# Row copies of k and q on other engines, and batch 0 ordered tile by tile, in an attention and feed-forward kernel

## The chip, the cores and the metric

The kernel runs on one NeuronCore of a Trainium2 chip. The core has TensorE (PE; PEld is its weight load), VectorE (DVE), ScalarE (ACT), GpSimd (POOL) and SyncE (SP), each with an instruction queue of its own that runs in order, and 16 DMA engines that all queues share. The metric is the device time of one execution in microseconds (us). The kernel before took a median of 387.32 us in three runs (386.34 to 393.78).

## What is computed

```python
# q, k, v: [8, 12, 448, 64] float32; w_in: [768, 2048]; w_out: [2048, 768]
scores = matmul(q, k.transpose(0, 1, 3, 2)) / sqrt(64) - log(448)
attn = 1 / (1 + exp(-scores))                  # a sigmoid, no softmax
x = matmul(attn, v).transpose(0, 2, 1, 3).reshape(8 * 448, 768)
h = x @ w_in
out = (h * (1 / (1 + exp(-h)))) @ w_out        # [3584, 768] float32
```

## The kernel before

**Quads, tiles, batches.** A quad is four of a batch's twelve heads, so there are 24 quads g, three (`NQ`) per batch. A quad has seven tiles (`NCH`) of 64 keys of each of its heads; `units` lists all 168 (g, ch) in order. For each tile `scores` (L171) makes four matmuls, with 64x64 of kT as weights and 448 columns of qT as the moving operand, into two PSUM banks (`psc`, two buffers in the pool `ps_sc`, L178), and then one sigmoid on ScalarE, 128x896, into `attnT` (L185). `values(g)` (L195) multiplies a quad's seven `attnT` tiles by v in 28 matmuls into two PSUM tiles `pav`, and VectorE writes them to `xT` (L220). A batch's feed-forward part needs the `xT` of its three quads.

**Feed-forward.** `h_unit(b, fc)` (L229) makes one of 16 tiles of h for a batch: six matmuls into `ph`, a sigmoid `tsig` on ScalarE (L245) and a multiplication `gTr` on VectorE (L246). The first four of the six need only the batch's first two quads. `out_set` (L286) multiplies two blocks of gTr by w_out with seven products in place of eight, with the sums and differences of blocks `S` (L315 to L323) and of quarters of w_out. The latter (`w_sums`, L264, L275) are 16 VectorE subtractions, 14 of which run one by one behind the h tiles 2 to 15 of batch 1. All of this is one generator, `stream`; each step is about one matmul and yields the time that it stands for.

**PSUM.** `ps_1` has four one-bank buffers for everything but the scores: `ph`, `po`, `pav`, `ptr` and the dummies `pw`.

**k and q transposed.** Scores need k and q with the head dimension on the partitions. Quads 0 to 5 are transposed by TensorE (`pe_transpose`, L141; 28 small matmuls against an identity, four pieces, each copied out of PSUM by VectorE, L156). Quads 6 to 23 go through `dma_transpose` (L160): GpSimd copies the rows of k and q into another order (`kr`, `qr`, 128x896 each, two buffers each in `p2`; L164), and SyncE issues a DMA transpose of each copy (L165). The results have four buffers in `p4`.

**Loads and stores.** GpSimd issues the loads of q, k, v and both weights, which change float32 to float16 on the way (L79, L109, L116). `kf` and `qf` have four buffers, `vf` five. SyncE issues nearly all stores of the output (L296).

**The loop (L473 to L505).** It walks over `units` in bursts of two tiles. Behind the burst's scores come the values of a quad whose last tile went by in an earlier burst, then perhaps the TensorE transposes of a quad to come, and then either dummy matmuls (`keep_busy`, in batch 0, up to four a burst; eight more run at the very start) or `stretch(ns)`, which takes steps from `stream` worth that many ns. Two h tiles of batch 0 are begun early (`early`, four matmuls each, L483 to L485). In front of tile 42, where batch 2 begins, one long `stretch(18500)` runs nearly all h tiles of batch 1. Loads and transposes by DMA hang on two hooks: `after_transpose(5)` makes the row copies of quads 6 and 7, `after_values(4)` those of quad 8, and `after_values(g)` from 5 on those of g + 4.

Of the kernel before, what the change touches and what calls it, by code (L numbers as in the profile page):

```python
# [10 lines left out]
F16 = mybir.dt.float16  # L11
# [6 lines left out]
def kernel(  # L18
# [9 lines left out]
    nc = tc.nc  # L28

    B, H, S, D = q.shape  # L30
    NT, DMODEL = out.shape
    DFF = moe_w_in.shape[1]
    P = 128
    HP = P // 2
    NCH = S // HP
# [36 lines left out]
    def load(names, g, c0=0, c1=NCH):  # L72
        b, iq = divmod(g, NQ)
        for name in names:
            if (name, g) not in flat:
                new_flat(name, g)
            for half in range(2):
                h0 = half * (H // 2) + 2 * iq
                nc.gpsimd.dma_start(  # L79
                    flat[name, g][half * HP : (half + 1) * HP, :, c0:c1].rearrange(  # L80
                        "p i c d -> p i (c d)"
                    ),
                    source[name][b, h0 : h0 + 2].rearrange("i (p c) d -> p i (c d)", c=NCH)[
                        :, :, c0 * D : c1 * D
                    ],
                )
# [38 lines left out]
    def new_qkT(g):  # L125
        for name in ("k", "q"):
            qkT[name, g] = p4.tile([P, NCH, P], F16, tag=f"{name}T", name=f"{name}T")
# [3 lines left out]
    def keep_busy(n):  # L131
        if n == 0:
            return
        pw = ps_1.tile([P, 512], F32, tag="ps1", name="pw")
        for _ in range(n):
            nc.tensor.matmul(pw, dummy[:, :P], dummy, start=True, stop=True)
# [4 lines left out]
    def pe_transpose(g, pieces=(("k", 0, 4), ("k", 4, NCH), ("q", 0, 4), ("q", 4, NCH))):  # L141
        if ("k", g) not in qkT:
            new_qkT(g)
        for name, c0, c1, *copy in pieces:
            dst = qkT[name, g].rearrange("p c t -> p (c t)")
            ptr = ps_1.tile([P, 512], F32, tag="ps1", name=f"ptr{name}")
            for c in range(c0, c1):
                for j in range(2):
                    nc.tensor.matmul(  # L149
                        ptr[j * D : (j + 1) * D, (c - c0) * P : (c - c0 + 1) * P],  # L150
                        flat[name, g][:, j, c, :],
                        ident,
                        start=True,
                        stop=True,
                    )
            (copy[0] if copy else nc.vector.tensor_copy)(  # L156
                dst[:, c0 * P : c1 * P], ptr[:, : (c1 - c0) * P]
            )

    def dma_transpose(g):  # L160
        new_qkT(g)
        for name in ("k", "q"):
            rows = p2.tile([P, NCH, 2, D], F16, tag=f"{name}r", name=f"{name}r")
            nc.gpsimd.tensor_copy(rows, flat[name, g].rearrange("p j c d -> p c j d"))  # L164
            nc.sync.dma_start_transpose(  # L165
                out=qkT[name, g], in_=rows.rearrange("p c j d -> p (c j d)")
            )

    attnT = {}

# [21 lines left out]

    part_of = {}

    def values(g, rounds=NCH):  # L195
        b, iq = divmod(g, NQ)
        if iq == 0:
            assert b < 2 or b - 2 in h_done
            xT[b] = p2.tile([P, NPAIR, S], F16, tag="xT", name="xT")
        pav, done_rounds = part_of.pop(g, None) or (  # L200
            [ps_1.tile([P, 512], F32, tag="ps1", name="pav") for _ in range(2)],
            0,
        )
        for ch in range(done_rounds, rounds):
            at = attnT.pop((g, ch))
            for half in range(2):
                own = slice(half * HP, (half + 1) * HP)
                for j in range(2):
                    nc.tensor.matmul(  # L209
                        pav[half][j * D : (j + 1) * D, :S],  # L210
                        flat["v", g][own, j, ch, :],
                        at[own, j, :],
                        start=(ch == 0),
                        stop=(ch == NCH - 1),
                    )
        if rounds < NCH:
            part_of[g] = pav, rounds
            return
        for half in range(2):
            nc.vector.tensor_scalar_mul(xT[b][:, half * NQ + iq, :], pav[half][:, :S], SX)  # L220
        if iq == NQ - 1:
            ready.add(b)
# [6 lines left out]
    def h_unit(b, fc):  # L229
        ph = ps_1.tile([P, 512], F32, tag="ps1", name="ph")  # L230
        for at, cc in enumerate(pairs):
            assert b in ready or at < 4
            nc.tensor.matmul(  # L233
                ph[:, :S],
                w_in_sb[:, cc, fc * P : (fc + 1) * P],
                xT[b][:, cc, :],
                start=(at == 0),
                stop=(at == NCC - 1),
            )
            if at < NCC - 1:  # L240
                yield 189
        if fc == NFC - 1:
            h_done.add(b)
        tsig = p3.tile([P, S], F16, tag="tsig", name="tsig")
        nc.scalar.activation(tsig, ph[:, :S], AF.Sigmoid, bias=0.0, scale=ISX)  # L245
        nc.vector.tensor_mul(  # L246
            gTr[:, fc, (b % 2) * S : (b % 2) * S + S], ph[:, :S], tsig
        )
        yield 189
# [36 lines left out]
    def out_set(a1, rows1, a2, rows2, last=False):  # L286
# [60 lines left out]
            store(rows1, osb[0], whole, (nc.sync, nc.sync))  # L347
        yield 163

    early = [h_unit(0, fc) for fc in range(2)]  # L350
    sums = w_sums()

    def moe_h(b):
        for fc in range(NFC):
            yield from early[fc] if b == 0 and fc < 2 else h_unit(b, fc)
            if b == 1 and fc >= 2:
                next(sums)

    def moe_set(m, g):
        step = out_set(block(g), row_blocks(m, g), block(g + 1), row_blocks(m, g + 1))  # L360
# [27 lines left out]
    def stretch(ns):  # L388
        nonlocal done, due
        due += ns  # L390
        while done < due:
            step_ns = next(stream, None)
            if step_ns is None:
                break
            done += step_ns
# [23 lines left out]
    def after_transpose(g):  # L419
        if g == 0:  # L420
            load("kq", 4)
            load_w_in(2)
            load("v", 3)
        elif g == 1:
            load("kq", 5)
            load_w_in(3)
            load("v", 4)
        elif g == 4:
            load("kq", 8)
            load("v", 6)  # L430
            load("v", 7)
        elif g == 5:
            load("v", 8)
            load("kq", 9)
            dma_transpose(6)
            dma_transpose(7)

    def after_values(g):
        if g == 0:
            load("v", 5)  # L440
            for nh in range(2):
                for part in range(2):
                    load_w_out(nh, part)
        elif g == 2:
            load("kq", 6)
            load("kq", 7)
        elif g == 4:
            load("kq", 10)
            load("kq", 11)
            dma_transpose(8)  # L450
            load("v", 9)
        elif g > 4:
            if g + 4 < NQB:
                dma_transpose(g + 4)
            if g + 5 < NQB:
                load("v", g + 5)
            if g + 7 < NQB:
                load("kq", g + 7)

    def values_if_any():  # L460
        if waiting:
            g = waiting.pop(0)
            values(g)
            after_values(g)
# [3 lines left out]
    keep_busy(1)  # L468
    pe_transpose(0, (("q", 0, 4), ("q", 4, NCH, act_copy), ("k", FIRST, NCH)))
    after_transpose(0)  # L470
    transposed = 1
    paces = {1: 1600, 2: 2200, 3: 2550, 4: 3400, 5: 3400, 6: 3000, 7: 3000}
    for n in range(0, len(units), 2):  # L473
        burst = units[n : n + 2]
        spare = 4 if n < 1.5 * NT_B else 0
        if n == 2 * NT_B:
            values_if_any()
            stretch(18500)
        elif n == NT_B + 1:
            values_if_any()  # L480
        for u in burst:
            scores(*u)
            if u[0] == NQ - 1 and u[1] >= NCH - 3 and u[1] % 2 == 0:  # L483
                for _ in range(4):
                    next(early[(u[1] - NCH + 3) // 2])  # L485
                if u[1] == NCH - 1:
                    values(u[0], NCH - 1)
        if waiting:
            spare = 0
        values_if_any()  # L490
        for g, ch in burst:
            if ch == NCH - 1:
                waiting.append(g)
        if transposed < 2 * NQ and n + 4 >= transposed * NCH - 1:
            pe_transpose(transposed)
            after_transpose(transposed)
            transposed += 1
            spare = 0
        if 0 not in ready:
            keep_busy(spare if n < NT_B - 3 else 0)  # L500
        else:
            stretch(paces[1] if 1 not in ready else paces[n // NT_B])
    for g in waiting:
        values(g)
    for _ in stream:  # L505
# [31 lines left out]
```

## Time and profile before

The profiled execution took 387.83 us; its span, from the first to the last instruction, is 386.1 us. All times below are of this execution.

| what | us |
|---|---|
| span | 386.1 |
| sigmoids of scores (L185), 168, mean 1005 ns | 159.5 busy on ACT |
| h matmuls (L233), 768 | 154.3 busy on PE |
| gTr (L246), 128, mean 622 ns | 77.8 busy on DVE |
| tsig (L245), 128, mean 546 ns | 67.6 busy on ACT |
| row copies (L164), 36, mean 1007 to 1035 ns by name (medians 1007 and 1006) | 37.0 busy on POOL |
| w_out differences (L275), 16 | 15.6 busy on DVE |
| issue of loads on POOL (L79), 144 | 88.2 |
| DMA transposes, issue to landing: least, median, most | 2.9, 3.3, 11.5 |

Lines of the profile name an engine, a line of the kernel, the tile written and the tile read, the shape and a count. A matmul's mean duration (353 ns for ph) is from its issue to its end; matmuls overlap, so the time that one takes in a row of them is read from a row's length over its count. In brackets stands how long the engine had been idle before, and what ended that. In a chain of waits each piece is what the next one waited for; "issue" is time for which the profile shows no wait. In tables by stretch each engine's busy time is followed by its number of instructions; the column behind POOL is the clock that the throttle granted to TensorE, 1.00 being full.

### The profile page before, as it was taken

The page shows a single profiled execution, that of the slowest core. Times are in us where ns is not written, and L with a number is a line of the kernel's source. Part 1 is how long each engine was busy: PE and PEld are TensorE (multiplying, and loading weights), DVE is VectorE, ACT ScalarE, POOL GpSimd, SP SyncE. Part 2 cuts the span into 40 slices and gives each one's busy share as a digit, 9 for nine tenths or more (in the row PEclk, how much of TensorE's full clock was granted, in tenths as well). Part 3 has the DMA queues.
Part 4 walks back from the last instruction along what each step waited for, and adds up shares of the span by engine and source line. Part 5 has one row for each costly group of instructions (what it writes and reads, how often), then busy time and mean ns, then how long its engine had stood idle before and what let it go on. Part 6 is the DMA issues. An engine that isn't in the chain of part 4 may idle for free.

```text
span 386.1 us, 7648 instructions
## 1 busy us (share of the span) xinstructions
PE 372.3 (96%) x3089; PEld 186.7 (48%) x3089; DVE 228.1 (59%) x385; ACT 235.4 (61%) x322; POOL 126.5 (33%) x194
## 2 busy tenths in 40 slices
PE   7898999879999999999999999999999999999995
PEld 2444444434554444544555544544455444555663
DVE  2445646998775446454667444644466445756774
ACT  4989885456865887577454487568774687044000
POOL 8937418954655514523505505303000000000000
PEclk9999999999999999999999999999999999999999
DMA  7999999999987937836569745452202300120233
GB/s 113 184 198 205 203 204 194 149 154 170 223 169 132 170 57 120 154 63 106 73 132 171 125 106 74 73 130 28 45 17 68 82 2 1 22 63 0 65 101 82
DMA packets 66403, 42.71 MB, mean 111 GB/s; under 512 B 37056, under 2 KB 62912, under 8 KB 66368
## 3 DMA queue, kind: packets, MB, share of 16 engines
q0 software_dynamic: 28032, 22.69, 40.6%
q1 hardware_dynamic: 38112, 19.31, 23.7%
q8 instruction: 24, 0.39, 0.4%
q10 hardware_dynamic: 224, 0.23, 0.2%
q14 instruction: 11, 0.09, 0.1%
HBM read 45.61 MB, written 11.01 MB: 147 GB/s over the span
## 4 chain that ended last, share of the span: by engine, by line
PE 86%; ACT 5%; DVE 5%; issue 2%; DMA 1%; POOL 1%; ACTq 0%; DVEq 0%; POOLq 0%
PE ph L233 34%; PE po L303 33%; PE psc L178 9%; PE pav L209 8%; ACT attnT L185 4%; DVE gTr L246 2%; DVE w_out_sb L275 1%; DVE T L275 1%; DMA kf<-in_k_dram 1%; ACT tsig L245 1%; DVE kT L156 0%; POOL qf L79 0%; PE ptrk L149 0%; DVE S L315 0%; DVE osb L311 0%
## 5 line engine op out<-in xcount | busy, mean ns | idle before, releaser
L185 ACT ACTIVATE attnT<-psc,bias_s 128x896 f16<-128x896 f32 x168 | 159.5, 1005 | 57.5 <-PE psc L178 57.2
L233 PE MATMUL ph<-xT,w_in_sb 128*128 128x448 f16 x768 | 154.3, 353 | 2.9 <-DVE gTr L246 2.7
L246 DVE TENSOR_TENSOR gTr<-ph,tsig 128x448 f16<-128x448 f32 x128 | 77.8, 622 | 82.3 <-ACT tsig L245 81.9
L233 PEld LDWEIGHTS <-w_in_sb 128*128 128x128 f16 x768 | 71.7, 98 | 79.8 <-issue 18.0
L245 ACT ACTIVATE tsig<-ph 128x448 f16<-128x448 f32 x128 | 67.6, 546 | 52.9 <-PE ph L233 48.7
L79 POOL DMA_DIRECT2D vf<-in_v_dram x48 | 28.9, 616 | 113.0 <-PE pav L209 69.4
L303 PEld LDWEIGHTS <-S 128*128 128x128 f16 x448 | 42.3, 98 | 34.1 <-issue 5.4
L311 DVE SCALAR_TENSOR_TENSOR osb<-po,osb 128x384 f32<-128x384 f32 x70 | 37.6, 554 | 27.4 <-PE po L303 27.2
L178 PE MATMUL psc<-qT,kT 64*64 64x448 f16 x672 | 50.2, 362 | 2.4 <-ACT attnT L185 2.0
L220 DVE TENSOR_SCALAR xT<-pav 128x448 f16<-128x448 f32 x48 | 27.7, 619 | 32.3 <-PE pav L209 32.3
L303 PE MATMUL po<-T,S 128*128 128x384 f16 x224 | 39.8, 326 | 0.9 <-DVE S L315 0.9
L303 PE MATMUL po<-w_out_sb,S 128*128 128x384 f16 x224 | 40.3, 326 | 0.0
L303 PEld LDWEIGHTS <-gTr 128*128 128x128 f16 x304 | 28.5, 98 | 23.8 <-issue 6.0
L209 PE MATMUL pav<-attnT,vf 64*64 64x448 f16 x672 | 36.5, 350 | 0.4 <-DVE gTr L246 0.4
L303 PE MATMUL po<-w_out_sb,gTr 128*128 128x384 f16 x192 | 34.7, 326 | 0.0
L79 POOL DMA_DIRECT2D kf<-in_k_dram x48 | 29.4, 635 | 9.4 <-PE ph L233 3.8
L79 POOL DMA_DIRECT2D qf<-in_q_dram x48 | 29.9, 654 | 7.5 <-PE ph L233 3.5
L178 PEld LDWEIGHTS <-kT 64*64 64x64 f16 x672 | 13.8, 104 | 32.9 <-issue 31.2
L209 PEld LDWEIGHTS <-vf 64*64 64x64 f16 x672 | 19.9, 107 | 12.8 <-issue 1.9
L311 DVE SCALAR_TENSOR_TENSOR osb<-po,m 128x384 f32<-128x384 f32 x42 | 23.1, 551 | 3.6 <-PE po L303 2.7
L318 ACT ACTIVATE m<-po 128x384 f32<-128x384 f32 x14 | 6.9, 492 | 24.2 <-PE po L303 23.7
L303 PE MATMUL po<-T,gTr 128*128 128x384 f16 x112 | 21.5, 327 | 0.0
(38 smaller groups left out, 157.0 us busy)
## 6 DMA issues: line engine op xcount, KB each, us to landing
out_dram<-osb SPq DMA_DIRECT2D x54, 192.0 KB, 3.0
qf<-in_q_dram POOLq DMA_DIRECT2D x48, 112.0 KB, 5.1
vf<-in_v_dram POOLq DMA_DIRECT2D x48, 112.0 KB, 4.3
kf<-in_k_dram POOLq DMA_DIRECT2D x46, 112.0 KB, 4.5
w_in_sb<-in_moe_w_in_dram POOLq DMA_DIRECT2D x4, 768.0 KB, 10.8
w_out_sb<-in_moe_w_out_dram POOLq DMA_DIRECT2D x4, 768.0 KB, 15.1
kT<-kr SPq DMA_TRANSPOSE x18, 3.3
qT<-qr SPq DMA_TRANSPOSE x18, 3.3
```

The lines of the kernel that those rows point to most:

```text
L79: nc.gpsimd.dma_start(flat[name, g][half * HP : (half + 1) * HP, :, c0:c1].rearrange("p i c d -> p i (c d)"), source[name][b, h0 : h0 + 2] ...
L178: nc.tensor.matmul(psc[own, j, :S], qkT["k", g][rows, ch, own], qkT["q", g][rows, :, own], start=True, stop=True,)
L185: nc.scalar.activation(attnT[g, ch], psc[:, :, :S], AF.Sigmoid, bias=bias_s, scale=QKSCALE)
L209: nc.tensor.matmul(pav[half][j * D : (j + 1) * D, :S], flat["v", g][own, j, ch, :], at[own, j, :], start=(ch == 0), stop=(ch == NCH - 1),)
L220: nc.vector.tensor_scalar_mul(xT[b][:, half * NQ + iq, :], pav[half][:, :S], SX)
L233: nc.tensor.matmul(ph[:, :S], w_in_sb[:, cc, fc * P : (fc + 1) * P], xT[b][:, cc, :], start=(at == 0), stop=(at == NCC - 1),)
L245: nc.scalar.activation(tsig, ph[:, :S], AF.Sigmoid, bias=0.0, scale=ISX)
L246: nc.vector.tensor_mul(gTr[:, fc, (b % 2) * S : (b % 2) * S + S], ph[:, :S], tsig)
L275: nc.vector.tensor_sub(o[:, f : f + 2], x[:, f : f + 2], y[:, f : f + 2])
L303: nc.tensor.matmul(po[:, :NO2], a[:, fc, :], w[:, fc, :], start=(fc == 0), stop=(fc == NHC - 1))
L311: nc.vector.scalar_tensor_tensor(out=o, in0=po, scalar=sign, in1=x, op0=ALU.mult, op1=ALU.add)
L318: nc.scalar.activation(m1, po, AF.Copy, scale=ISX)
```

## The change

- `dma_transpose` takes a quad, one of the two names and the copy to use. GpSimd makes no row copies any more.
- Quads 6, 7 and 8 are copied by ScalarE, k and q one after the other, behind the h tiles 4, 7 and 10 of batch 1 (`by_h1`), with the load of k and q of the quad four on behind each pair.
- Quads 9 to 23 are copied by VectorE. From `after_values(6)` on they are put on a list, `later`, and each burst takes one copy from it, behind the burst's values; the load of k and q of the quad four on follows the copy of q.
- The first 24 tiles are no longer run in bursts of two. Behind the scores of each tile stands what a table, `behind`, lists for it: dummies, the transposes of k or of q of a quad, two or three tiles' share of a quad's values, or two matmuls of an early h tile. The transposes of quads 1 to 3 come ahead of the values of quads 0 to 2. `values` can stop at any tile and go on later, as before. Behind tile 23 a stretch follows, and then the loop of two-tile bursts as before. The loop's dummies in batch 0 go from 16 to 9.

```diff
-    def dma_transpose(g):
-        new_qkT(g)
-        for name in ("k", "q"):
-            rows = p2.tile([P, NCH, 2, D], F16, tag=f"{name}r", name=f"{name}r")
-            nc.gpsimd.tensor_copy(rows, flat[name, g].rearrange("p j c d -> p c j d"))
-            nc.sync.dma_start_transpose(
-                out=qkT[name, g], in_=rows.rearrange("p c j d -> p (c j d)")
-            )
+    def dma_transpose(g, name, copy):
+        if ("k", g) not in qkT:
+            new_qkT(g)
+        rows = p2.tile([P, NCH, 2, D], F16, tag=f"{name}r", name=f"{name}r")
+        copy(rows, flat[name, g].rearrange("p j c d -> p c j d"))
+        nc.sync.dma_start_transpose(
+            out=qkT[name, g], in_=rows.rearrange("p c j d -> p (c j d)")
+        )
...
+    by_h1 = {4: 6, 7: 7, 10: 8}
...
     def moe_h(b):
         for fc in range(NFC):
             yield from early[fc] if b == 0 and fc < 2 else h_unit(b, fc)
-            if b == 1 and fc >= 2:
-                next(sums)
+            if b == 1:
+                if fc >= 2:
+                    next(sums)
+                if fc in by_h1:
+                    for name in ("k", "q"):
+                        dma_transpose(by_h1[fc], name, act_copy)
+                    load("kq", by_h1[fc] + 4)
...
     def after_transpose(g):
...
         elif g == 5:
             load("v", 8)
             load("kq", 9)
-            dma_transpose(6)
-            dma_transpose(7)
...
     def after_values(g):
...
-        elif g == 4:
-            load("kq", 10)
-            load("kq", 11)
-            dma_transpose(8)
-            load("v", 9)
-        elif g > 4:
-            if g + 4 < NQB:
-                dma_transpose(g + 4)
-            if g + 5 < NQB:
-                load("v", g + 5)
-            if g + 7 < NQB:
-                load("kq", g + 7)
+        elif g >= 4 and g + 5 < NQB:
+            load("v", g + 5)
+        if g >= 6:
+            for to in (9, 10) if g == 6 else (g + 4,):
+                if to < NQB:
+                    later.extend(((to, "k"), (to, "q")))
+
+    later = []
+
+    def rows_if_any():
+        if later:
+            g, name = later.pop(0)
+            dma_transpose(g, name, nc.vector.tensor_copy)
+            if name == "q" and g + 4 < NQB:
+                load("kq", g + 4)
...
+    behind = {
+        1: ((keep_busy, 2),),
+        2: ((keep_busy, 1),),
+        3: ((transposes, 1, "k"),),
+        4: ((transposes, 1, "q"),),
+        5: ((keep_busy, 2),),
+        6: ((keep_busy, 2),),
+        7: ((keep_busy, 2),),
+        8: ((transposes, 2, "k"),),
+        9: ((transposes, 2, "q"),),
+        10: ((rounds, 0, 2),),
+        11: ((rounds, 0, 4),),
+        12: ((rounds, 0, 7),),
+        13: ((transposes, 3, "k"),),
+        14: ((transposes, 3, "q"),),
+        15: ((rounds, 1, 2),),
+        16: ((rounds, 1, 4),),
+        17: ((rounds, 1, 7),),
+        18: ((begin, 0),),
+        19: ((begin, 1),),
+        20: ((rounds, 2, 2),),
+        21: ((begin, 0), (rounds, 2, 4)),
+        22: ((rounds, 2, 7),),
+        23: ((begin, 1),),
+    }
+    for n in range(NT_B + 3):
+        scores(*units[n])
+        for do, *what in behind.get(n, ()):
+            do(*what)
+
+    transposed = NQ + 1
     paces = {1: 1600, 2: 2200, 3: 2550, 4: 3400, 5: 3400, 6: 3000, 7: 3000}
-    for n in range(0, len(units), 2):
+    stretch(paces[1])
+    for n in range(NT_B + 3, len(units), 2):
         burst = units[n : n + 2]
-        spare = 4 if n < 1.5 * NT_B else 0
         if n == 2 * NT_B:
             values_if_any()
             stretch(18500)
-        elif n == NT_B + 1:
-            values_if_any()
         for u in burst:
             scores(*u)
-            if u[0] == NQ - 1 and u[1] >= NCH - 3 and u[1] % 2 == 0:
-                for _ in range(4):
-                    next(early[(u[1] - NCH + 3) // 2])
-                if u[1] == NCH - 1:
-                    values(u[0], NCH - 1)
-        if waiting:
-            spare = 0
         values_if_any()
+        rows_if_any()
```

`transposes` calls `pe_transpose` for the two pieces of one name and, behind q, `after_transpose`; `rounds(g, end)` is `values(g, end)`, with `after_values(g)` at the end of a quad; `begin(fc)` takes two steps of an early h tile.

More of the change, by code (lines that the diff above doesn't have):

```diff
@@ L193, with values @@
     part_of = {}
-    def values(g, rounds=NCH):
+    def values(g, end=NCH):
         b, iq = divmod(g, NQ)
-        if iq == 0:
+        if b not in xT:
             assert b < 2 or b - 2 in h_done
@@ L203, in values @@
         )
-        for ch in range(done_rounds, rounds):
+        for ch in range(done_rounds, end):
             at = attnT.pop((g, ch))
@@ L215, in values @@
                     )
-        if rounds < NCH:
-            part_of[g] = pav, rounds
+        if end < NCH:
+            part_of[g] = pav, end
             return
@@ L470, with transposes, rounds, begin @@
     after_transpose(0)
-    transposed = 1
+    def transposes(g, name):
+        pe_transpose(g, ((name, 0, 4), (name, 4, NCH)))
+        if name == "q":
+            after_transpose(g)
+    def rounds(g, end):
+        values(g, end)
+        if end == NCH:
+            after_values(g)
+    def begin(fc):
+        for _ in range(2):
+            next(early[fc])
+    behind = {
[28 more added lines that the diff above has]
+    transposed = NQ + 1
     paces = {1: 1600, 2: 2200, 3: 2550, 4: 3400, 5: 3400, 6: 3000, 7: 3000}
-    for n in range(0, len(units), 2):
+    stretch(paces[1])
+    for n in range(NT_B + 3, len(units), 2):
         burst = units[n : n + 2]
-        spare = 4 if n < 1.5 * NT_B else 0
         if n == 2 * NT_B:
@@ L497 @@
             transposed += 1
[L498 to L502, printed above, removed]
+        stretch(paces[1] if 1 not in ready else paces[n // NT_B])
     for g in waiting:
```

## The prediction, made before the changed kernel ran

> **What bounds the kernel now.** I read the page's busy times first, then busy times by stretch, then the chain of waits, then the order in time of the two places where the stretches show a hole. Times are microseconds. The profiled execution took 387.83: its span of 386.1 and 1.73 around it. It is 0.5 over the median of the runs shown, 387.32, and inside their 386.34 to 393.78; the sum below is made on 387.83.
>
> ```profile
> PE 372.3 (96%) x3089; PEld 186.7 (48%) x3089; DVE 228.1 (59%) x385; ACT 235.4 (61%) x322; POOL 126.5 (33%) x194
> ```
>
> TensorE is busy for 96% of the span, no other engine for over 61%. By stretch (busy time of PE, PEld, DVE, ACT, POOL, then clock and DMA):
>
> ```profile
> 7.80:31.80 24.00, 21.63 (x296) 10.76 (x292) 10.12 (x19) 22.68 (x26) 16.55 (x27) 1.00 1.21 188
> 59.80:86.70 26.90, 23.29 (x136) 11.26 (x133) 25.15 (x36) 13.23 (x22) 22.66 (x34) 1.00 1.33 164
> 86.70:381.90 295.20, 295.13 (x2336) 149.73 (x2336) 175.00 (x301) 173.38 (x240) 69.89 (x103) 1.00 0.48 90
> ```
>
> From 86.7 on TensorE has 0.07 of idle time in 295.20: nothing can be won there by waits, and whatever starts the last stretch earlier ends the kernel earlier by as much. The holes are batch 0 (ACT is busy 22.68 of 24.00) and 59.8 to 86.7 (VectorE is busy 25.15 of 26.90). The chain of waits in the second (start, length, what):
>
> ```profile
> 59.83 7.50 PE ph L233 x39
> ...
> 68.55 0.55 DVE T L275
> 69.10 3.11 issue
> 72.21 0.61 DVE gTr L246
> ...
> 76.32 2.44 DVE w_out_sb L275
> ...
> 86.01 0.61 DVE S L315
> ...
> 86.67 1.83 PE po L303 x10
> ```
>
> From 67.9 to 86.67 the chain runs on VectorE. The order in time says why:
>
> ```profile
> 68.21 1.05 POOL L164 COPY kr<-kf 128x896 f16<-128x896 f16 x1
> 68.47 3.81 DVE L275 TENSOR_TENSOR T<-w_out_sb 128x768 f16<-128x768 f16 x1
> 72.87 4.80 PE L233 MATMUL ph<-xT,w_in_sb 128*128 128x448 f16 x24 [1.02 <-DVE gTr L246]
> 76.24 2.52 DVE L275 TENSOR_TENSOR w_out_sb<-w_out_sb 128x768 f16<-128x768 f16 x1
> 76.37 1.11 POOL L164 COPY kr<-kf 128x896 f16<-128x896 f16 x1
> 79.35 2.24 PE L233 MATMUL ph<-xT,w_in_sb 128*128 128x448 f16 x11 [1.68 <-DVE gTr L246]
> ```
>
> A subtraction that takes 0.54 elsewhere takes 3.81 while GpSimd makes four row copies in a row (68.21 to 71.86), and 2.52 beside the next two; TensorE then waits 1.02 and 1.68 for gTr. In batch 0:
>
> ```profile
> 7.83 9.19 ACT L185 ACTIVATE attnT<-psc,bias_s 128x896 f16<-128x896 f32 x10 [0.61 <-PE psc L178]
> 28.61 2.80 ACT L185 ACTIVATE attnT<-psc,bias_s 128x896 f16<-128x896 f32 x3 [0.85 <-PE psc L178]
> 28.73 1.16 DVE L220 TENSOR_SCALAR xT<-pav 128x448 f16<-128x448 f32 x2 [2.76 <-PE pav L209]
> 31.79 0.57 PE L178 MATMUL psc<-qT,kT 64*64 64x448 f16 x8
> ```
>
> Ten sigmoids run back to back at 0.919; 24 of them from 7.83 would end at 29.89, and end at 31.41. ACT lost 1.52 to scores that came late, and the h matmuls wait for xT, ready at 29.89.
>
> **Row copies away from GpSimd.** From 59.83 to 86.67 TensorE has this work: 99 ph matmuls at 0.189 (96 in 18.16 late in the chain) = 18.71, 16 po at 0.163 (168 in 27.31) = 2.61, two score groups at 0.50 = 1.00, and four changes between them at 0.11 (18 ph beside scores take 3.51 against 3.40) = 0.44; together 22.8 of 26.84. The hole is worth 4.1 and is the most that this edit can give. It opens fully only if VectorE keeps up: without GpSimd's copies its turn per h tile is gTr 0.54 and the subtraction 0.47 in the chain, 1.01 against six matmuls = 1.13. It does, by a tenth.
>
> In the place of GpSimd's ten copies in this stretch come six on ACT, ahead of the tsig of tiles 5, 8 and 11 of h(1). ACT copies of this shape are not in the trace. Nearest: 128x512 from SBUF 0.632 (L364), and from L245's 448 elements in 0.546 to L185's 896 in 1.005 it is 1.02 ns an element; so an estimate of 1.02, and 0.93 behind another, as the sigmoids overlap: 1.95 a pair. Behind the pair wait tsig, then gTr, then the PSUM buffer that TensorE needs. A tile takes 1.2 from its last matmul to the end of gTr (0.54 and 0.62, with gaps), and its buffer is needed again after three more tiles, 3.4: cover for 2.2. One pair fits. Per three tiles ACT has 1.95 and three tsig at some 0.5, 3.45 against 3.4, so the three pairs hardly add up; with VectorE catching up I charge 0.4, and 0.2 for S (L315) behind the last gTr. Bounds: nothing, and all three pairs uncovered, 5.9. I stay near the low end because the cover is counted from rows. Term: 4.1 - 0.6 = **3.5**.
>
> SP has the transposes of quads 6 to 8 at once before the stores; quad 6's first landed after 3.9. Quad 6 is copied near 66 and its scores come near 78, so some 6 are spare. kq 10 to 12 on POOL now wait for the ACT copies; behind them are only loads for later batches.
>
> Thirty copies go to VectorE after 90, one a burst, after xT. Their price is not in the trace: 428 ns for 128x512 from f32 (L414) below, GpSimd's 1007 above; 0.5 taken, 15 in all of 295 with VectorE at 175. TensorE waits for VectorE in none of that stretch, so this counts nothing; uncovered it would be at most 30 times 0.5. What sits behind each copy is a gTr or osb whose buffer has three more tiles of time. In return the S additions lose GpSimd (L323 1033 ns between 90 and 270, 681 after it); also off the path. A copy waits for the transposes of two quads before, which landed within 11.5; the quads are some 14 apart.
>
> A rule speaks against VectorE here. The Trainium skill (SBUF — State Buffer, "SBUF: two separate sides") says that a VectorE copy in a two-port mode locks GpSimd out, so that a DMA issued there stretches from about 620 to 3100 ns. By that, as an estimate, thirty copies could cost POOL 74; no run here shows it, and the sum would stay as it is, since POOL is idle for two thirds of the span.
>
> **Batch 0 tile by tile.** Transposes of quads 1 to 3, values and early h matmuls are the same work, one piece behind each tile's scores. The largest usual piece, 12 value matmuls at 47 ns (28 in 1.32) = 0.57, with scores at 0.25 makes 0.82 of the sigmoid's 0.919; one place (two h matmuls and eight values) is some 0.1 over, covered by the second score buffer. So ACT should run unbroken. Scores of tile 22 then start when sigmoid 20 ends, 7.83 + 21 x 0.919 = 27.13; with 0.38 and 0.57 the values end at 28.08, xT 1.2 later at 29.3 against 29.89; one of the nine h matmuls that waited now goes ahead. The scores of tile 24 come at 30.9 or so, not 31.79. Term: **0.8**; bounds 1.5 (all that ACT lost) and -1.0 (as many new late scores as before). Loads allow it: w_in's first quarter, issued at 13.73 and landed 8.8 later, is needed at 23.9. Sixteen dummies of the loop become nine; they only fill.
>
> From 31.8 to 59.8 and after 86.7 the order of the path is as before. Sum: 387.83 - 3.5 - 0.8 = **383.5**.
>
> **Rivals.** *ACT takes GpSimd's place.* If a pair takes over 2.2 (1.1 a copy), TensorE waits instead; wholly uncovered the stretch takes 22.8 + 5.9 = 28.7 against 26.84, and with 0.8 from batch 0 the time is 388.9, slower than before. For it: ACT's balance is 3.45 to 3.4. Against: four buffers. 13%.
>
> *The clock.* The first eight dummies take 3.26, 0.41 each; from 7.90 four take 1.04, though the clock reads 1.00 in both. If fewer dummies bring that rate back in batch 0, a piece of 0.82 becomes 1.64, 0.7 over the sigmoid, in some 17 tiles: +12, 399. It decides once matmuls of batch 0 run at twice their time. Against: real work takes the dummies' place at much the same density. 4%. The Trainium skill (TensorE: Matmul & The Clock Gate, Part 1) has half rate return after an idle window of some 3.4; by that the price would be nothing, as no hole in the plan is so long.
>
> *Half an effect.* VectorE's margin of 0.12 a tile is spent on late tsig, so that the chain stays on it, or batch 0's new order loses what it gains: 385.5 to 387.8. 18%.
>
> *More.* Over 2% needs 8, and the holes hold 4.1 + 1.5; only something unseen gives it. 5%.
>
> **How the numbers follow.** The forecast has 60%, 383.5 (382.2 to 385 for its own bounds). Eight in ten: from 381.0 (near all of both holes, and a run 0.5 quicker, as the median is) to 387.6. Two per cent of 387.32 is 7.7, about what this measurement tells from no change: faster 5%, slower 6% (the clock, and a bad end of the ACT case), within 89%.
>
> **What would show it.** L275 at some 0.55 a piece with no 2 to 4 among them; no TensorE wait for gTr over 0.5 between 59 and 83; 24 sigmoids in one run from 7.8 to about 30; POOL busy some 37 less; ACT copies at 1.0. Wrong if TensorE waits for tsig beside the ACT copies, if 60 to 87 still takes over 25, or if scores wait in batch 0.

## The result, and the profile after

The changed kernel takes a median of 389.9 us (17 runs, 386.64 to 391.57) beside 387.53 for the kernel before (17 runs): a ratio of 1.0054, 95% interval 1.0032 to 1.0077. It is slower, by 2.1 us by this ratio, where the prediction had 383.5, 3.8 below the median that it knew. Ratios leave out executions over 1.5% above the fastest of their kernel; medians do not. The profiled execution took 390.17 with a span of 388.4. Every difference between two spans below is one between single profiled executions; medians and ratios are from the timed runs.

Busy times of the changed kernel, on its page:

```profile
PE 374.1 (96%) x3082; PEld 186.9 (48%) x3082; DVE 232.5 (60%) x415; ACT 239.9 (62%) x328; POOL 93.5 (24%) x158
```

GpSimd is busy 33 less, nearly the 37 that left it. TensorE does seven dummies fewer and is busy 1.8 longer, so some matmuls ran slower. The table by stretch, with the columns as before (the last three are clock, DMA share and GB/s):

```profile
7.80:31.80 24.00, 22.07 (x290) 10.40 (x288) 10.92 (x20) 22.77 (x26) 14.84 (x25) 1.00 1.20 184
59.80:86.70 26.90, 22.08 (x112) 10.48 (x111) 16.21 (x31) 15.27 (x25) 16.64 (x28) 0.87 1.30 145
80.00:82.00 2.00, 0.09 (x1) 0.09 (x1) 0.77 (x2) 2.00 (x5) 2.00 (x4) 0.50 1.53 102
84.00:86.00 2.00, 2.00 (x12) 0.64 (x9) 1.33 (x3) 1.49 (x2) 0.60 (x1) 0.50 1.79 93
89.10:384.20 295.10, 295.09 (x2337) 149.82 (x2335) 185.42 (x330) 174.63 (x241) 42.98 (x73) 1.00 0.58 91
```

In the second stretch VectorE fell from 25.15 to 16.21, as the change meant. Yet TensorE is busy less than before there, with a hole around 80, and its clock is 0.50 at the end of the hole and behind it. The last stretch is as long as before and as full: all of the loss is made before 89.1. The order in time, ACT, VectorE and TensorE together:

```profile
70.47 0.94 ACT L139 ACTIVATE qr<-qf 128x896 f16<-128x896 f16 x1
74.87 0.95 ACT L139 ACTIVATE kr<-kf 128x896 f16<-128x896 f16 x1 [1.73 <-DMA kT<-kr]
79.82 0.95 ACT L139 ACTIVATE qr<-qf 128x896 f16<-128x896 f16 x1 [4.00 <-DMA qT<-qr]
81.23 0.62 DVE L246 TENSOR_TENSOR gTr<-ph,tsig 128x448 f16<-128x448 f32 x1 [6.27 <-ACT tsig L245]
81.91 2.02 PE L233 MATMUL ph<-xT,w_in_sb 128*128 128x448 f16 x5 [4.82 <-DVE gTr L246]
85.11 2.87 PE L303 MATMUL po<-w_out_sb,gTr 128*128 128x384 f16 x12
89.07 1.79 PE L303 MATMUL po<-T,S 128*128 128x384 f16 x10
```

Read from the top: ScalarE copies quads 6 and 7 without a wait, and then stands twice in front of quad 8's copies until a DMA transpose has read the buffer that the copy is to write (`kr` and `qr` have two buffers each, so quad 8 writes where quad 6 stood). The tsig of four h tiles queue behind, VectorE has no tsig to multiply by for 6.27, all four PSUM buffers of `ph` are full, and TensorE stands for 4.82. Twelve `po` then take 2.87 where they take 2.11 at full clock. The product that opened the last stretch at 86.67 before opens it at 89.07: 2.4 later, and the span is 2.3 longer.

The transposes' side, SyncE and GpSimd from 66 on (a transpose's duration is that of its issue):

```profile
67.19 1.30 SPq L165 DMA_TRANSPOSE kT<-kr  x1
67.81 1.29 POOL L79 DMA_DIRECT2D kf<-in_k_dram  x2
68.58 2.40 SPq L165 DMA_TRANSPOSE qT<-qr  x1
69.17 1.20 POOL L79 DMA_DIRECT2D qf<-in_q_dram  x2
70.33 1.22 POOL L79 DMA_DIRECT2D vf<-in_v_dram  x2
71.09 3.46 SPq L165 DMA_TRANSPOSE kT<-kr  x1
74.64 4.57 SPq L165 DMA_TRANSPOSE qT<-qr  x1
```

The first two landed 7.6 and 11.1 after their issue; the one issued first in the kernel before, at 69.29, landed after 3.9. Loads are issued between them here. Before, the only work of GpSimd from 68.21 to 71.71 was four row copies, and its loads stood behind those. Once those loads ran again, transposes landed late there too: the ones issued at 72.05 and 73.39 after 7.6 and 11.0.

### The profile page after: what moved, and what is told of

Same layout as the page of the kernel before. It is cut to its first block, busy times and chain, and to the rows that moved or that the text cites. A ratio compares the mean times of both kernels' runs of the same rounds, so it can differ in the third digit from the quotient of the medians.

```text
span 388.4 us, 7660 instructions
## 1 busy us (share of the span) xinstructions
PE 374.1 (96%) x3082; PEld 186.9 (48%) x3082; DVE 232.5 (60%) x415; ACT 239.9 (62%) x328; POOL 93.5 (24%) x158
## 4 chain that ended last, share of the span: by engine, by line
PE 79%; DMA 13%; POOL 5%; issue 1%; DVE 1%; ACT 0%; ACTq 0%; POOLq 0%
PE po L303 34%; PE ph L233 30%; PE psc L178 8%; PE pav L209 7%; DMA w_out_sb<-in_moe_w_out_dram 4%; DMA vf<-in_v_dram 3%; DMA qT<-qr 3%; DMA w_in_sb<-in_moe_w_in_dram 3%; POOL qf L79 2%; POOL kf L79 2%; POOL vf L79 1%; DVE xT L220 0%; POOL w_in_sb L109 0%; DVE gTr L246 0%; DVE osb L311 0%
## 5 line engine op out<-in xcount | busy, mean ns | idle before, releaser
L303 PEld LDWEIGHTS <-S 128*128 128x128 f16 x448 | 42.5, 98 | 32.9 <-issue 6.1
L303 PEld LDWEIGHTS <-gTr 128*128 128x128 f16 x304 | 28.8, 99 | 24.2 <-issue 6.6
L303 PE MATMUL po<-w_out_sb,S 128*128 128x384 f16 x224 | 40.3, 326 | 0.0
L303 PE MATMUL po<-T,S 128*128 128x384 f16 x224 | 39.8, 326 | 0.0
L209 PE MATMUL pav<-attnT,vf 64*64 64x448 f16 x672 | 38.2, 350 | 0.8 <-DVE gTr L246 0.4
L79 POOL DMA_DIRECT2D qf<-in_q_dram x48 | 29.0, 617 | 29.2 <-DVE qr L164 15.2
L303 PE MATMUL po<-w_out_sb,gTr 128*128 128x384 f16 x192 | 35.5, 331 | 0.0
L178 PEld LDWEIGHTS <-kT 64*64 64x64 f16 x672 | 14.9, 105 | 32.1 <-issue 30.4
L303 PE MATMUL po<-T,gTr 128*128 128x384 f16 x112 | 21.5, 327 | 0.0
```

The lines of the kernel that those rows point to most:

```text
L79: nc.gpsimd.dma_start(flat[name, g][half * HP : (half + 1) * HP, :, c0:c1].rearrange("p i c d -> p i (c d)"), source[name][b, h0 : h0 + 2] ...
L178: nc.tensor.matmul(psc[own, j, :S], qkT["k", g][rows, ch, own], qkT["q", g][rows, :, own], start=True, stop=True,)
L209: nc.tensor.matmul(pav[half][j * D : (j + 1) * D, :S], flat["v", g][own, j, ch, :], at[own, j, :], start=(ch == 0), stop=(ch == NCH - 1),)
L303: nc.tensor.matmul(po[:, :NO2], a[:, fc, :], w[:, fc, :], start=(fc == 0), stop=(fc == NHC - 1))
```

## The experiments

The theory was that (a) the loss is ScalarE's wait for the buffers of quad 8, with the halved clock behind it; (b) the transposes are late because loads run beside them; and (c) the rest of the change gains what was forecast. The rivals: the copies themselves take tsig's place (the rival on record); VectorE's thirty copies or batch 0 lose it. Each edit is against the changed kernel, and none leaves any of its work out.

**A third row buffer.**

```diff
-        rows = p2.tile([P, NCH, 2, D], F16, tag=f"{name}r", name=f"{name}r")
+        rows = p3.tile([P, NCH, 2, D], F16, tag=f"{name}r", name=f"{name}r")
```

> The changed kernel with three row buffers for each of kr and qr in place of two, so that no copy of quad 8 waits for a transpose of quad 6. In the profile of the changed kernel ScalarE waited 1.7 and 4.0 us for those buffers, TensorE 4.8 us behind it, and the clock stood at half from about 79 to 86. Theory A (the buffers are the cause): these waits and the half clock are gone, the seven products of the first output set start where the plan had them, some 5 to 7 us earlier than 89.1, and the kernel takes 383 to 385. Theory B (the transposes are late themselves, whoever waits for them): q of quad 6 landed at 79.7 and its scores were planned near 78, so TensorE waits there instead, 1.8 us or more, and the time is 385 to 388. Theory C (the ScalarE copies' own time holds TensorE): waits of TensorE for gTr stay, 389 to 390.

385.44 (10 runs; before 387.14), ratio 0.9966 (0.9935 to 0.9997): one buffer turns the loss into a gain of 1.7. TensorE in the order of time of the profiled execution (388.01, one of the longer of the ten), and a stretch of it:

```profile
78.18 0.57 PE L178 MATMUL psc<-qT,kT 64*64 64x448 f16 x8 [1.00 <-DMA qT<-qr]
82.73 1.83 PE L303 MATMUL po<-T,S 128*128 128x384 f16 x10 [0.47 <-DVE S L315]
89.85 0.38 PE L178 MATMUL psc<-qT,kT 64*64 64x448 f16 x4 [2.26 <-DMA qT<-qr]
90.40 3.90 PE L303 MATMUL po<-w_out_sb,S 128*128 128x384 f16 x13
```

```profile
90.26:93.68 3.42, 3.42 (x12) 1.61 (x12) 1.04 (x3) 1.01 (x1) 0.26 (x1) 0.50 1.38 101
```

The product comes 6.3 earlier than in the changed kernel, with all six copies still on ScalarE. What is late next is the transposes themselves: scores of quads 6 and 7 wait for qT. Behind the second of these waits the clock is 0.50 for 3.42, and thirteen `po` take 3.90, where they take 2.28 in `two_act` below.

**The loads later in the program.**

```diff
-                    load("kq", by_h1[fc] + 4)
...
-        elif g >= 4 and g + 5 < NQB:
+        elif g > 6 and g + 5 < NQB:
             load("v", g + 5)
         if g >= 6:
+            if g == 6:
+                for to in (10, 11, 12):
+                    load("kq", to)
+                for to in (9, 10, 11):
+                    load("v", to)
```

> The changed kernel with two row buffers as it is, but the loads of k and q of quads 10 to 12 and of v of quads 9 to 11 are issued behind the values of quad 6, after the long stretch of batch 1. Theory A1 (the transposes are late because they share the DMA engines with these loads): the transposes of quads 6 to 8 land within 8 us in place of 7.6 to 15.2, ScalarE's wait for the buffers shrinks under 1 us, 383 to 386. Theory A2 (they are late whatever else moves, from the issue and from each other): they still take 10 us and more, and the time stays at 388 to 390.

388.87 (9 runs), ratio 1.005 (1.0017 to 1.0082), no cure. ScalarE still waits 2.50 and 3.56, and quad 6's transposes land after 8.3 and 11.5. GpSimd's queue shows why it tells nothing of (b): loads fill it from 66.95 to 72.28 with gaps of 0.27 at most, since those of quad 9 and of v 7 and 8 had stayed, and nothing stands in front of a later load on that queue but other loads. A later place in the program held nothing back.

**A hold by order of loads.** At h tile 10 of batch 1 the load of k and q of quad 12, which must wait for ScalarE's copy of quad 8, is put in front of v 7 to 10 and of quads 9 to 11; with two row buffers (`gate`) and with three (`gate3`).

```diff
+                    if fc == 10:
+                        for g in (9, 10, 11):
+                            for name in ("k", "q"):
+                                new_flat(name, g)
+                        load("kq", 12)
+                        load("v", 7)
+                        load("kq", 9)
...
```

> The changed kernel with two row buffers, and with the loads that were in the DMA engines beside the transposes of quads 6 to 8 really held back: on GpSimd's queue the load of k and q of quad 12, which must wait for ScalarE's copy of quad 8, now comes first, and behind it v of 7 to 10 and k and q of 9 to 11. (In the run with later places for these loads GpSimd had gone ahead all the same: the k and q loads were issued from 72.7 on, and only those of v 9 to 11 moved, from near 70 to 83; the transposes still took up to 15.9.) Theory A1 (the transposes are late because the loads share the DMA engines): quads 6 to 8 land within 6 us each, ScalarE waits less than 1 us for row buffers, TensorE's wait of 5 and the half clock are gone, 383 to 385. Theory A2 (the transposes hold up each other): landing stays over 10, 387 to 390.

> The loads held back as in the run beside it, and three row buffers too. Theory A1: the third buffer has nothing left to do, the same time as with two buffers within 0.7 us, 383 to 385. Theory A2: as with three buffers alone, 385.4, with waits of the scores for the transposes of q of quads 6 and 7 (1.0 and 2.3 us there).

`gate` 389.17 (10 runs; before 387.19), ratio 1.0038 (1.0009 to 1.0066); `gate3` 386.3 (10 runs), 0.9953 (0.9919 to 0.9987). The profiled execution of `gate` took 386.17, the shortest of its ten. Even in it the hold failed: loads go on without a gap of more than 1.7 from 59.45 to 83.60, and quad 6's transposes land after 7.6 and 9.1. Quad 12 waited only for ScalarE's copy at 67. So the pair says nothing on (b), and once more what the buffer is worth: 2.9.

**A hold by data.** GpSimd copies two elements of gTr of h tile 10, which it must wait for, in front of the loads (`held`); `held3` adds the third buffer.

```diff
+    hold = cpool.tile([P, 2], F16, tag="hold", name="hold")
...
-                    load("kq", by_h1[fc] + 4)
+                if fc == 12:
+                    nc.gpsimd.tensor_copy(hold, gTr[:, 10, S : S + 2])
+                    for g in (9, 10, 11, 12):
+                        load("kq", g)
+                        load("v", g - 2)
...
```

> The changed kernel with two row buffers. On GpSimd's queue a copy of two elements of h tile 10 of batch 1 stands in front of the loads of k and q of quads 9 to 12 and of v of 7 to 10, so that none of them is issued before that tile is done, near 73.5. (In the run called gate the tile framework gave quad 12 a buffer that was free, its load did not wait, and loads ran at 63.7 to 72 as before: that run held nothing back.) Theory A1 (the transposes are late because loads share the DMA engines): kT and qT of quads 6 and 7 land within 5 us, as the first two did in the kernel before (3.9 and 3.8), ScalarE waits under 0.5 us for a row buffer, TensorE does not wait for gTr, 383 to 384.5. Theory A2 (six transposes hold up each other): they still take 8 and more, 387 to 390.

> The same with three row buffers. A1: within 0.5 of the run beside it. A2: 385 to 386.5, as three buffers gave before.

`held` 386.06 (10 runs; before 387.02), ratio 0.9969 (0.9945 to 0.9994); `held3` 385.04 (6 runs), 0.9939 (0.9894 to 0.9984). `held` in order of time, TensorE, ScalarE and GpSimd:

```profile
58.97 18.71 PE L233 MATMUL ph<-xT,w_in_sb 128*128 128x448 f16 x98
72.67 0.94 ACT L139 ACTIVATE kr<-kf 128x896 f16<-128x896 f16 x1
73.51 0.94 ACT L139 ACTIVATE qr<-qf 128x896 f16<-128x896 f16 x1
74.20 0.45 POOL L366 COPY hold<-gTr 128x2 f16<-128x2 f16 x1 [8.54 <-DVE gTr L246]
77.61 0.57 PE L178 MATMUL psc<-qT,kT 64*64 64x448 f16 x8
82.17 1.82 PE L303 MATMUL po<-T,S 128*128 128x384 f16 x10 [0.48 <-DVE S L315]
```

With no load issued from 65.7 to 74.7 the first five transposes land after 2.9 to 4.2; the sixth, issued at 74.95 with the loads running again, after 7.4. Still with two buffers, ScalarE waits for none, all six copies lie in cover, and 98 h matmuls run without a gap. That shows (b), and it refutes that three pairs of ScalarE copies are too many. The time is still above the 383 to 384.5 that was expected: the product comes 4.5 earlier than before, but the end only 1.7. By stretch, `held`:

```profile
100.00:120.00 20.00, 18.74 (x173) 9.54 (x166) 12.58 (x23) 11.51 (x13) 8.29 (x14) 1.00 1.32 148
120.00:140.00 20.00, 18.92 (x153) 8.42 (x155) 9.79 (x18) 15.39 (x24) 4.73 (x8) 1.00 1.35 144
```

TensorE lacks 1.26 and 1.08 there, where the kernel before and the changed one are full (20.00 in both stretches), at a DMA share of 1.32 and 1.35 against 0.90 and 0.83 before. The chain of waits names it:

```profile
98.93 18.69 DMA kT<-kr
...
117.74 0.06 DVE kr L164
...
118.27 15.94 DMA qT<-qr
...
134.33 0.62 DVE qr L164
134.95 0.54 DVE gTr L246
...
135.54 0.73 PE ph L233 x3
```

The held loads run on beside later transposes, which now land after 18.69 and 15.94, and VectorE's copies wait for their two buffers as ScalarE's had: 1.5 and 11.5 in all by the page's groups, 0.0 with the third buffer in `held3`. It is the same wait on the other engine. The third buffer does not make the transposes land sooner: in `held3` TensorE itself waits 1.47 for a qT at 134.54.

**Quad 8 alone.** Its two copies go from ScalarE to the head of VectorE's list; loads as in the changed kernel, two buffers.

```diff
-    by_h1 = {4: 6, 7: 7, 10: 8}
+    by_h1 = {4: 6, 7: 7}
...
+                if fc == 10:
+                    later.extend(((8, "k"), (8, "q")))
```

> The changed kernel, but quad 8's two copies are taken from ScalarE and given to VectorE, as the first two on its list: they are made in the first two bursts behind the long stretch (near 79 and 82), when quad 6's transposes have landed (74.8 and 79.7 in the changed kernel). ScalarE keeps the four copies of quads 6 and 7, which have free buffers. All loads stay where they are, so the transposes still land late. Theory (the loss of the changed kernel is the wait of ScalarE for the two buffers in front of quad 8's copies, and the clock behind it; four copies on ScalarE cost next to nothing): no TensorE wait for gTr over 0.5 between 59 and 78, the clock 1.00, third product near 82.2 as with the loads held; scores of quad 6 or 7 may wait for qT by up to some 2, as with three buffers, and quad 8's too, since its transposes start 5 to 8 later. Time 384 to 386. Rival (ScalarE's copies themselves take tsig's place, whatever the buffers): with four of six copies left, two thirds of the 4.8 hole stays, third product 85 to 87, time 387 to 389. Rival (VectorE's copy waits for the transposes and holds gTr and xT behind it): a TensorE wait for gTr or pav of 1 or more beside 79 to 84, time 386 to 388.

386.45 (12 runs, 384.24 to 387.63; before 387.21), ratio 0.9978 (0.9953 to 1.0002), just over the 384 to 386 expected; the profiled execution took 384.24, the shortest of the twelve. TensorE and VectorE in its order of time:

```profile
59.15 18.71 PE L233 MATMUL ph<-xT,w_in_sb 128*128 128x448 f16 x98
78.71 0.61 DVE L164 COPY kr<-kf 128x896 f16<-128x896 f16 x1
82.52 1.83 PE L303 MATMUL po<-T,S 128*128 128x384 f16 x10 [0.48 <-DVE S L315]
84.18 0.61 DVE L164 COPY qr<-qf 128x896 f16<-128x896 f16 x1
87.77 0.38 PE L178 MATMUL psc<-qT,kT 64*64 64x448 f16 x4 [0.39 <-DMA qT<-qr]
```

Transposes land as late as ever (7.4 to 14.8 for quads 6 and 7), but nothing of tsig stands behind a copy that waits for one, and the hole is gone. That shows (a), with four copies on ScalarE; `rows3` and `held` show it with all six. In this execution the time is 3.6 below the profile of before; the median is only 0.8 below, within its noise. No longer execution was profiled; what the clocks on record say of them stands under "Left open".

**The clock by itself.** Twenty dummies, into a buffer of the scores, ahead of the last h tile of batch 1, to fill the hole.

```diff
+            if b == 1 and fc == NFC - 1:
+                pw = ps_sc.tile([P, 2, 512], F32, tag="pssc", name="pw2")
+                for _ in range(20):
+                    nc.tensor.matmul(pw[:, 0], dummy[:, :P], dummy, start=True, stop=True)
```

> The changed kernel with 20 dummy matmuls, which write into a score buffer that nobody reads, ahead of the last h tile of batch 1, where TensorE stood idle for 4.8 us. They take 20 x 0.213 = 4.3 us of the hole. If the half clock behind the hole cost time of its own (from the trace, the matmuls between 81.9 and 87 took some 2.5 us longer than elsewhere), the clock stays at 1.00 and the kernel gets 1.5 to 2.5 us faster than the changed one: 387 to 388.5. If the hole alone is the loss, it stays within 0.5 of it: 389.4 to 390.4.

389.75 (4 runs), ratio 1.0106 (1.0074 to 1.0139): no gain in time. `warm` from 75 to 91 by stretch, and in order of time:

```profile
75.00:91.00 16.00, 13.63 (x88) 6.03 (x86) 8.29 (x16) 8.55 (x13) 4.79 (x9) 1.00 1.49 117
```

```profile
76.55 4.48 PE L360 MATMUL pw<-dummy 128*128 128x512 f16 x20
82.92 1.10 PE L233 MATMUL ph<-xT,w_in_sb 128*128 128x448 f16 x5 [1.89 <-DVE gTr L246]
84.66 2.11 PE L303 MATMUL po<-w_out_sb,gTr 128*128 128x384 f16 x12
88.51 1.83 PE L303 MATMUL po<-T,S 128*128 128x384 f16 x10 [0.48 <-DVE S L315]
```

The clock stays at 1.00, and from the end of the hole to the product it takes 5.59 instead of 7.16, so the halved clock costs 1.57 in the changed kernel. But h went on 1.0 later (82.92 against 81.91), which left 0.6 in this execution and nothing in the median. So keeping the clock up did not cure the hole here.

**Parts of the change.** `b0_only`: batch 0 tile by tile, all row copies back on GpSimd at their old places. `rows_only`: the row copies of the change, batch 0 as before. `dve_rest`: batch 0 tile by tile, quads 6 to 8 on GpSimd as before, 9 to 23 on VectorE as in the change; its core:

```diff
+    def pool_rows(g):
+        for name in ("k", "q"):
+            dma_transpose(g, name, nc.gpsimd.tensor_copy)
...
-                if fc in by_h1:
-                    for name in ("k", "q"):
-                        dma_transpose(by_h1[fc], name, act_copy)
-                    load("kq", by_h1[fc] + 4)
...
             load("kq", 9)
+            pool_rows(6)
+            pool_rows(7)
...
+        elif g == 4:
+            load("kq", 10)
+            load("kq", 11)
+            pool_rows(8)
+            load("v", 9)
```

> Batch 0 tile by tile as in the changed kernel; all row copies on GpSimd with their transposes and loads where the kernel before had them. By the profile of the changed kernel batch 0 brings 0.2 to 0.5 us (its tile 24 starts at 31.55 against 31.79, its long stretch at 59.33 against 59.76), so 386.8 to 387.4. By the prediction 0.8: 386.7. If the new order of batch 0 is itself a loss, more than 388.

> The row copies of the changed kernel (ScalarE for 6 to 8, VectorE for 9 to 23), with batch 0 in bursts of two as in the kernel before. If the two parts add up: changed kernel 389.9, less the gain of batch 0 alone (387.14 - 385.73 = 1.4) taken back, 390.5 to 391.5. If batch 0's earlier end is what makes the transposes collide with the loads, then less, 387 to 389.

> Batch 0 tile by tile; quads 6 to 8 copied by GpSimd where the kernel before did it; quads 9 to 23 copied by VectorE, one copy a burst, as in the changed kernel. Against the run with all copies on GpSimd (385.73) only the thirty copies of 0.61 us on VectorE differ. If they cost nothing, as predicted, 385.2 to 386.3; a little less if quad 9's GpSimd copy, now gone, had held up the sums in the long stretch's end (VectorE's S behind it waited 2.4 us there). If VectorE's queue is where the loss is, 387 or more.

| kernel | us (runs), before beside it | ratio (95%) |
|---|---|---|
| b0_only | 385.73 (10), 387.14 | 0.9966 (0.9935 to 0.9997) |
| rows_only | 390.23 (10), 387.19 | 1.006 (1.0029 to 1.0091) |
| dve_rest | **384.8** (9), 387.19 | 0.9942 (0.9919 to 0.9965) |

Batch 0 gains, the row copies lose, and within them the thirty copies on VectorE lose nothing that shows: the median of `dve_rest` is 0.9 below that of `b0_only`, though their intervals overlap. The six on ScalarE cost the whole: 389.9 against 384.8. The parts do not quite add up: `rows_only` is only 0.3 above the changed kernel, below the 390.5 to 391.5 expected. `dve_rest` beats both kernels (its own lines stand 4 later: L279 is L275, L307 is L303), though GpSimd's copies still stretch VectorE's subtraction there, as its order in time shows:

```profile
68.40 4.06 DVE L279 TENSOR_TENSOR w_out_sb<-w_out_sb 128x768 f16<-128x768 f16 x1
73.04 5.80 PE L237 MATMUL ph<-xT,w_in_sb 128*128 128x448 f16 x29 [1.26 <-DVE gTr L250]
83.34 1.83 PE L307 MATMUL po<-T,S 128*128 128x384 f16 x10 [0.48 <-DVE S L319]
```

## Why the prediction was wrong

**The step that failed** is the one on SyncE's queue: "quad 6's first landed after 3.9 … so some 6 are spare". Two things were wrong in it. It took the landing from the one place of the profile where GpSimd's own copies kept loads out of the way, though quad 7's two landed after 7.6 and 11.0 in that same profile; with those copies gone loads run on, and quad 6's two land after 7.6 and 11.1 as well. And it counted only the scores as waiting for a landing. The row buffer waits too: the sentence "a copy waits for the transposes of two quads before" was written for VectorE's copies, 14 apart, and not for ScalarE's, which are 3.4 apart and stand in front of tsig. With two buffers quad 8's copies, due near 73, could not be made before 74.87 and 79.82.

The price adds up. From the start of the long stretch to the product the changed kernel takes 89.07 - 59.33 = 29.74, and with quad 8 elsewhere 82.52 - 59.15 = 23.37. The difference of 6.37 is the hole, 4.82, and the clock, 1.57 (together 6.39).

**Row copies, 4.1 - 0.6 = 3.5.** Without the failed step the term was right. In `two_act` and `held` 98 h matmuls take the 18.71 that was counted for 99, and from the start of the long stretch to the product `two_act` takes 23.37, against 22.8 + 0.6 = 23.4 counted. Its product comes 86.67 - 82.52 = 4.15 earlier than before, batch 0 included, against 4.3 forecast. L275 takes 548 ns with no long one left. Within the 0.6 the parts were off: TensorE waits 0.48 for S, where 0.2 was charged, and for tsig it never waits in those two kernels, where the copies were charged 0.4; they take 0.94 each (estimate 1.02). In the changed kernel the charge came to 29.74 - 22.8 = 6.9 in place of 0.6, and the 6.4 between this and `two_act` is the failed step's.

**VectorE's thirty copies.** 609 ns each, inside the bounds of 0.43 to 1.0 and above the 0.5 taken; free, as stated: TensorE has 0.01 of idle time in 295.10, and `dve_rest` shows no loss. The S additions of L323 take 681 ns now that GpSimd copies nothing, as forecast.

**Batch 0, 0.8.** Right in size: `b0_only` has a span 0.9 below that of before, and a median 1.4 below, with an interval from nearly 0 to 2.5. In the profile of the changed kernel the long stretch begins only 0.4 earlier (59.33 against 59.76). The sigmoids of the changed kernel and the wait that breaks them (order in time, then the chain of waits), and last the sigmoids of `b0_only`:

```profile
7.61 19.07 ACT L185 ACTIVATE attnT<-psc,bias_s 128x896 f16<-128x896 f32 x21 [0.61 <-PE psc L178]
25.83 0.93 PE L209 MATMUL pav<-attnT,vf 64*64 64x448 f16 x8 [0.38 <-DMA vf<-in_v_dram]
```

```profile
15.10 10.69 DMA vf<-in_v_dram
```

```profile
7.91 21.70 ACT L189 ACTIVATE attnT<-psc,bias_s 128x896 f16<-128x896 f32 x24 [0.66 <-PE psc L182]
```

In `b0_only`, as in nine of the eleven profiles with the new order, all 24 run unbroken, as the prediction said. In the changed kernel's profile 21 do. Then values of quad 2 stand for v, which lands at 25.79; "Loads allow it" had looked at w_in alone. In the eleventh, `held`, it is w_in that lands late, by 0.77.

**The rivals.** "ACT takes GpSimd's place" is what happened by its sign (TensorE waits for tsig beside ScalarE's copies) and nearly by its time, 388.9 against a profiled 390.17. Its reason and its point of decision are refuted: a copy takes 0.94, not over 1.1, so that its time came near is luck. "The clock" came, at another place and price: 0.50 from 79.8 to 86.6 and 1.57, not 12 in batch 0, where the clock is 1.00. The two-port rule of the Trainium skill (SBUF — State Buffer, "SBUF: two separate sides") did not show: thirty VectorE copies left the loads' issue as it was (617 ns a q load against 654 before), and GpSimd is busy 33 less, where the estimate by that page was 74 more. Whether these copies ran in such a mode no run shows. The range of 381.0 to 387.6 ended below 388.9, the time of the rival that came.

**Left open**: why the median of `two_act` is 2.2 above its profiled execution. The mean clock on record for each execution tells a part. In seven of the twelve it is 0.994 to 0.996, with a median of 386.6; in the other five it is 0.999 or 1.000, with a median of 385.6. In `rows3` the four executions below 0.997 took 385.51 or more and the other six 383.50 to 385.62. The profile of `rows3` is one of its four: 3.42 at half clock, behind a wait for a late qT, put the mean over a span of 386.2 at 0.996. The long executions of `two_act` may lose time in the same way, but none was profiled, and the rest of the 2.2 has no explanation.

## What to carry to other kernels

When a step moves to another engine, its waits move too, and they must be looked up on the old engine, where nobody may have minded them: the kernel before had this wait already, 3.0 on GpSimd, with only loads behind it.

```profile
L164 POOL COPY qr<-qf 128x896 f16<-128x896 f16 x18 | 18.6, 1035 | 3.0 <-DMA qT<-qr 3.0
```

For every instruction put on an engine that feeds the bottleneck, check when its output buffer comes free, and take that time from a profile in which the same transfers run beside it. A slow engine that does the old work may be what spaces the transfers out, as GpSimd's row copies were here.

## What the runs showed of the hardware

- A DMA transpose of 128x896 lands, counted from its issue, after 2.9 to 4.2 with no loads issued beside it (`held`, the first five) and after 7.4 to 15.2 among loads (`two_act` and the changed kernel), at the same place of nearly the same program. Over all 36 transposes the page of the changed kernel gives medians of 6.0 and 5.7, that of before 3.3 and 3.3.
- TensorE's clock halved behind holes of 3.86 (`rows_only`: 12 `po` in 2.57), 4.82 and 5.14 (`late`), but also behind one of 2.26 (`rows3`), and not behind one of 2.74 (`gate`: five h matmuls in 1.10, the time they take at full clock in `warm`). So the length of the hole alone does not decide. In the traces the clock changes only at whole multiples of 3.41 from one another. Cut into such stretches, TensorE was busy for 1.15 of 3.41 in the one ahead of the drop in `rows3`, for 0.70 in the changed kernel, 0.37 in `rows_only` and 0.06 in `late`; in `gate`, where the clock stayed, the least is 1.47. `rows3`, then `gate`:

```profile
86.85:90.26 3.41, 1.15 (x12) 0.39 (x11) 0.75 (x2) 1.01 (x1) 1.18 (x2) 1.00 1.45 113
75.24:78.65 3.41, 1.47 (x8) 0.67 (x7) 0.00 (x0) 1.54 (x4) 1.52 (x3) 1.00 1.31 175
```

The Trainium skill (TensorE: Matmul & The Clock Gate, Part 1) has half rate come after an idle window of some 3.4. The length of the window agrees with these traces; that it must be idle does not, since TensorE worked for a third of the one in `rows3`.

- A row of four copies by GpSimd stretched a VectorE subtraction from 0.55 to 3.81 (before), 4.06 (`dve_rest`) and 4.55 (`b0_only`), while copies by VectorE did nothing that shows to GpSimd's issue of loads.
